# New states from 40 instead of 64 columns of keys, and two fixed double banks in PSUM

## The chip, the cores and the metric

The kernel runs on one core of a Trainium2 chip. The metric is the device time of one execution in microseconds (us). The engines are named as in the profile: PE is TensorE's matrix product, PEld its weight load (of the stationary operand), DVE is VectorE, ACT is ScalarE, POOL is GpSimd, SP is SyncE, which issues most of the DMAs. L602 is line 602 of the kernel before the change; in the changed kernel the lines after L337 stand three further down.

## The reference, cut to what matters

Two blocks follow each other. The first is an mLSTM cell over 4 batches x 8 heads (32 heads in all), 768 steps and a head width D of 40; the second a two-layer network with a quick GELU on the 3072 x 320 result.

```python
for t in range(S):                                   # per head; C is 40 x 40, n is 40
    m_new  = maximum(f_gate[t] + m, i_gate[t])
    f_stab = exp(f_gate[t] + m - m_new)
    i_stab = exp(i_gate[t] - m_new)
    C = f_stab * C + i_stab * outer(v[t], k[t])      # the state
    n = f_stab * n + i_stab * k[t]
    y[t] = sigmoid(o[t]) * (C @ q[t]) / maximum(abs(n . q[t]), 1)
x = y as (3072, 320)
h = x @ w_in                                         # w_in is 320 x 2048
out = (h * sigmoid(1.702 * h)) @ w_out               # w_out is 2048 x 320
```

All tensors are fp32.

## The kernel before

**Windows.** The 768 steps are cut into six windows of 128 steps. Within a window the cell is computed as masked attention: `scores` (L445 to L462) multiplies queries and keys into `p_s`, `weights` makes the decay factors `wt`, `values` (L485 to L519) multiplies scores by the values into `p_o` and adds in `p_i` what the state from the windows before contributes. `carry` (L595 to L612) makes the new state: for every head it multiplies the keys, transposed, by the scaled values `vw` into `p_c`, and VectorE adds that to the decayed old state. The values have one column more than D (D1 = 41, a column of ones), so the state carries C and n together.

**The state's layout.** Two heads share a column block of the state: the even head stands on partitions 0 to 39, the odd head on 64 to 103, with room for 64 each (DP = 64). In `carry` the keys are the stationary operand and the 41 columns of `vw` the moving one, so the number of key columns is the number of PSUM partitions written. The 24 columns behind a head's 40 are zeros in windows 0 and 1; from window 2 on the keys are stored densely (`k_st`) and the 24 columns are the first ones of the next head. Nothing reads what they produce: `values` takes rows 0 to 39 of each half.

**Products on tiles.** A window after the first is held in two halves of 64 steps, and the odd heads' halves are swapped, so the products of `scores`, `values` and `carry` stand on four tiles of 64 rows x 64 columns of TensorE's array, one after the other (`slot(i, x)`). `carry` of window 0 has 128 rows of keys and uses two tiles of 128 x 64. In window 5 only the first half's state is wanted, and its two products a head pair stand on two of the four tiles. An fp32 product shows as two rows of PE and two of PEld in the trace.

**Order.** Instructions are issued in the order of the program on each engine; a framework adds the semaphore waits between engines. `attention(w)` places the steps of the next window between the 16 or 14 blocks of the second product of the current one (`down` at L790, `down_fast` at L844): `carry` of both groups of 16 heads (c = 0 and c = 1) after block 3, `scores` of both some blocks later, `values` of each group in a block's place of its own, then `seam_out`, `seam_in` and `seam_turn`, which bring the result y through DRAM into the layout of the network's input xT. The first product follows (`up` at L626 and L635 in window 0, `up_fast` at L701 and L722 after it).

**PSUM.** The eight banks are two pools: `ps_m` with four single banks, and `ps_a` with two double banks. `banks(name)` at L337 takes a double bank: for the transposes `p_t`, for `p_w`, `p_cols`, `p_x`, `p_c`, `p_s`, `p_o`, `p_i` and for two pairs of rows of `p_h`. In the kernel before each call makes a new tile of the pool. Such a tile gets the double bank that was freed first, and its first writer waits until every access to the tile that had it is over.

Of the kernel before, what the change touches and what calls it, by code (L numbers as in the profile page):

```python
# [8 lines left out]
FP = mybir.dt.float32  # L9
# [17 lines left out]
def kernel(  # L27
# [13 lines left out]
    B, H, S, D = q.shape  # L41
# [6 lines left out]
    D1 = D + 1  # L48
    DP = 64
# [4 lines left out]
    PH = 2 * H  # L54
# [11 lines left out]
    ps_a = ctx.enter_context(tc.tile_pool(name="ps_a", bufs=2, space=PSUM))  # L66
# [3 lines left out]
    V, A, G, T = nc.vector, nc.scalar, nc.gpsimd, nc.tensor  # L70
# [3 lines left out]
    k_st = const.tile([L, BH * D + DP - D], FP, name="k_st")  # L74
# [20 lines left out]
    def k_of(w):  # L95
        return (k_0, k_1)[w] if w < 2 else k_st[:, 0:BH * D].rearrange("s (h d) -> s h d", d=D)

    def k_cols(w, t, h):

        return k_of(w)[t, h, :] if w < 2 else k_st[t, h * D:h * D + DP]  # L100

    def load_squares(w, what):
        for dst, src in [((k_sq, k), (q_sq, q))["kq".index(c)] for c in what]:
# [229 lines left out]
    def slot(i, x):  # L333

        return slice((x ^ i) * HL, (x ^ i) * HL + HL)

    def banks(name):  # L337
        return ps_a.tile([128, 2, 512], FP, tag="a", name=name)

    def masks():  # L340
        V.tensor_reduce(out=odd, in_=full.rearrange("p (j two) -> p two j", two=2)[:, 1], axis=AX.X, op=OP.add)
# [17 lines left out]
    def columns(w):  # L359
        if w == 0:  # L360
            pt = banks("p_cols")[:, 0, :]
            T.transpose(pt[:, 0:3 * BH], stacked[w], full)
            c = cols[w] = gate.tile([L, 4 * BH], FP, name="cols")
            A.activation(out=c[:, 2 * BH:3 * BH], in_=pt[:, 2 * BH:3 * BH], func=AF.Exp, scale=-1.0)
            return
        c = cols[w]
        A.activation(out=c[:, BH:3 * BH], in_=c[:, BH:3 * BH], func=AF.Exp, scale=-1.0)
        d = raw[w][:, 3 * BH:].rearrange("p (j i x) -> p i x j", i=2, x=2)
        for i in range(2):
            r = slice(i * 64, i * 64 + 64)  # L370
            A.activation(out=c[r, 3 * BH:].rearrange("p (x j) -> p x j", x=2), in_=d[r, i], func=AF.Exp)
# [4 lines left out]
    def transposes(w, b, between=None):  # L376
        both = ((kT, "kT", k_of(w)), (qT, "qT", q_st))[:1 if w else 2]
        for dst, name, _ in both:
            dst[w, b] = work.tile([128, NP, L], FP, tag=name, bufs=4, name=name)
        pt = banks("p_t")  # L380
        for x, (_, _, src) in enumerate(both):
            if x and between:
                between()
            for p in range(NP):
                h = b * H + 2 * p
                T.transpose(pt[:, x, p * L:(p + 1) * L], src[:, h:h + 2, :].rearrange("p a b -> p (a b)"), ident)  # L386
        for x, (dst, _, _) in enumerate(both):
            A.copy(out=dst[w, b].rearrange("r j t -> r (j t)"), in_=pt[:, x, :])
# [19 lines left out]
    def weights_begin(c):  # L408
        if c:
            both = banks("p_w")  # L410
            p_w[c] = [both[:, i, :].rearrange("s (p t) -> s p t", t=L) for i in range(2)]
        else:
            p_w[c] = [ps_m.tile([L, NP, L], FP, tag="m", name="p_w") for _ in range(2)]
        for i in range(2):
            T.matmul(p_w[c][i], ident_b, neg_mask.unsqueeze(1).to_broadcast([L, NP, L]), start=True, stop=False)
# [158 lines left out]
    def decay(w, c, x, engine=G):  # L574

        js = slice(c * NJ, (c + 1) * NJ)
        d = cols[w][:, 3 * BH + x * BH // 2:3 * BH + (x + 1) * BH // 2][:, js]
        old, dst = ((state[w % 2], state_mid), (state_mid, state[1 - w % 2]))[x]
        engine.tensor_tensor(out=dst[:, js], in0=old[:, js], in1=d.unsqueeze(2).to_broadcast([128, NJ, D1]),
                             op=OP.mult)  # L580
# [13 lines left out]
    def carry(w, c):  # L594
        js = slice(c * NJ, (c + 1) * NJ)  # L595
        pc = banks("p_c")
        n = 2 if 0 < w < NW - 1 else 1
        for j in range(NJ):
            for i in range(2):
                for x in range(n):  # L600
                    t = slot(i, x) if w else slice(0, L)
                    T.matmul(pc[i * 64:i * 64 + 64, x, j * D1:(j + 1) * D1], k_cols(w, t, c * PH + 2 * j + i),  # L602
                             vw[w, c][t, 2 * j + i, :], start=True, stop=True)
        new = lambda x: pc[:, x, 0:NJ * D1].rearrange("r (j d) -> r j d", d=D1)
        if w == 0:
            A.copy(out=state[1][:, js], in_=new(0))
            return
        for x, dst in enumerate((state_mid, state[1 - w % 2])[:n]):
            if x:
                decay(w, c, x, V)  # L610
            V.tensor_tensor(out=dst[:, js], in0=new(x), in1=dst[:, js], op=OP.add)
# [306 lines left out]
    def attention(w):  # L918
        at = (0, 1, 3, 3, 5, 6, 8, 8, 9, 12, 14) if w == 1 else (0, 0, 1, 3, 1, 4, 5, 6, 6, 10, 11)
        calls = [[(columns, w), (scale, w, 0), (scale, w, 1), (decay, w, 0, 0), (decay, w, 1, 0)],  # L920
                 [(weights, w, 0)], [(weights, w, 1)], [(carry, w, 0), (carry, w, 1)], [(open_gates, w)],
                 [(scores, w, 0), (scores, w, 1)], [(values, w, 0)], [(seam_out, w, 0), (seam_in, w, 0)],
                 [(values, w, 1), (seam_out, w, 1), (seam_in, w, 1)], [(seam_turn, w, 0)], [(seam_turn, w, 1)]]
        side = {}
        for i, c in zip(at, calls):
            side.setdefault(i, []).extend(c)
        return side

    for w in range(NW):
        more = w + 1 < NW  # L930
        if w == 0:
            for j in range(NF // 2):
                if j % 2 == 0:
                    ahead, behind = converted[j // 2]
                    run([(convert, p) for p in ahead] + [(fetch, p) for p in fetched.get(j // 2, ())])
                    up(w, j, lambda: run([(columns_turn, 1) if p is None else (convert, p) for p in behind]))
                if j == 6:
                    load(1, "o")
                if j == 1:
                    wait_for(w_in_sb[:, 1, 512:1024])  # L940
                    scale(0, 1)
                    load(1, "v")
                if j < B and j % 2:
                    carry(0, j // 2)
                if j == 3:
                    masks()
                    gates(1)
                    columns_in(1)
                if j == 4:
                    spread(1)  # L950
                    load_squares(1, "q")
                if j >= B:
                    transposes(1, j - B)
# [78 lines left out]
```

## Time and profile before

| what | us |
| --- | --- |
| time before, median of 3 runs (466.46 to 466.73) | 466.53 |
| span of the profiled execution, from the first to the last instruction | 464.1 |
| what lies around the span, by the difference of the two | 2.4 |
| PE busy (98% of the span) | 456.6 |
| PEld busy (84%) | 391.2 |
| DVE busy (75%) | 349.2 |
| ACT busy (40%) | 185.8 |
| POOL busy (35%) | 162.8 |
| mean granted TensorE clock, as a share of full speed | 0.996 |

The profile gives the profiled execution by its span alone, and a sum made against it is carried over to the median by the 2.4 us around it. The runs agree within 0.3 us. Busy time of an engine counts every moment in which at least one of its instructions runs; PE's matmuls overlap, so many short ones on several tiles count once. An engine's idle time costs only where the chain that ends last goes through it.

### The profile page before, as it was taken

What the parts mean: (1) busy time and instruction counts of PE and PEld (TensorE: products, weight loads), DVE (VectorE), ACT (ScalarE), POOL (GpSimd) and SP (SyncE); (2) the same over time, 40 slices, a digit from 0 to 9 for tenths busy, and PEclk for the clock granted to TensorE, in tenths of its full rate; (3) what the DMA queues carried; (4) which work ended last, traced back from release to release, by engine and by line L of the source; (5) the groups of instructions that cost most, each with busy time, mean ns of one, the idle gap of its engine ahead of it and who ended that gap; (6) DMA issues with size and microseconds to landing.
All of it is one profiled execution on the core that took longest, in us unless ns stands there. A gap on an engine that the chain in (4) does not pass through costs nothing.

```text
span 464.1 us, 12384 instructions
## 1 busy us (share of the span) xinstructions
PE 456.6 (98%) x5071; PEld 391.2 (84%) x5071; DVE 349.2 (75%) x738; ACT 185.8 (40%) x433; POOL 162.8 (35%) x154
## 2 busy tenths in 40 slices
PE   8999999999989999999999999999999999999996
PEld 6867877776859999779999779999888999787996
DVE  6788998799958785888786888787788766553722
ACT  5686779000536700455800354900264910164200
POOL 5101508000797700266800167610157710146200
PEclk9999999999989999999999999999999999999999
DMA  8998999049976025969024978315999305000000
GB/s 169 187 295 187 253 239 204 4 106 198 149 157 78 3 59 123 200 113 189 9 58 107 194 119 162 53 33 125 175 140 156 63 18 140 29 1 1 1 28 30
DMA packets 135561, 52.87 MB, mean 114 GB/s; under 512 B 101984, under 2 KB 131632, under 8 KB 135504
## 3 DMA queue, kind: packets, MB, share of 16 engines
q1 hardware_dynamic: 127136, 50.27, 55.4%
q10 hardware_dynamic: 8048, 1.66, 1.8%
q8 instruction: 40, 0.66, 0.6%
q0 software_dynamic: 320, 0.15, 0.2%
q14 instruction: 17, 0.14, 0.1%
HBM read 44.52 MB, written 7.54 MB: 112 GB/s over the span
## 4 chain that ended last, share of the span: by engine, by line
PE 88%; SPq 4%; DMA 2%; issue 2%; DVE 2%; POOL 1%; ACT 1%; DVEq 0%; POOLq 0%; ACTq 0%
PE p_out L844 33%; PE p_h L722 24%; PE p_out L790 8%; PE p_h L701 7%; PE p_h L626 5%; SPq L122 3%; PE p_c L602 3%; PE p_o L503 2%; PE p_s L459 2%; PE p_i L511 2%; DMA s_in<-in_moe_w_in_dram 2%; PE p_h L635 2%; POOL g L781 1%; SPq L167 0%; PE p_t L386 0%
## 5 line engine op out<-in xcount | busy, mean ns | idle before, releaser
L781 POOL TENSOR_TENSOR g<-g,parts 128x512 f32<-128x512 f32 x30 | 38.2, 1272 | 196.5 <-ACT g L739 187.7
L761 ACT COPY parts<-p_h 128x256 f32<-128x256 f32 x40 | 14.9, 372 | 164.5 <-PE p_h L722 134.1
L844 PE MATMUL p_out<-w_out_sb,g 128*128 128x160 f32 x480 | 68.9, 300 | 0.0
L722 PE MATMUL p_h<-xT,w_in_sb 128*128 128x256 f32 x240 | 66.4, 385 | 2.0 <-ACT g L739 2.0
L844 PEld LDWEIGHTS p_out<-w_out_sb,g 128*128 128x128 f32 x480 | 66.4, 190 | 0.5
L690 ACT ACTIVATE g<-g 128x512 f32<-128x512 f32 x80 | 47.8, 629 | 30.1 <-DVE g L775 19.1
L722 PEld LDWEIGHTS p_h<-xT,w_in_sb 128*128 128x128 f32 x240 | 44.9, 191 | 14.2 <-issue 5.5
L849 DVE TENSOR_TENSOR o_sb<-o_sb,p_out 128x160 f32<-128x160 f32 x70 | 21.4, 317 | 44.2 <-PE p_out L844 43.6
L844 PE MATMUL p_out<-t_sb,s 128*128 128x160 f32 x320 | 47.1, 300 | 0.0
L844 PEld LDWEIGHTS p_out<-t_sb,s 128*128 128x128 f32 x320 | 44.4, 190 | 0.2
L722 PE MATMUL p_h<-t_x,s_in 128*128 128x256 f32 x160 | 42.0, 385 | 0.0
L435 ACT ACTIVATE wt<-wt,cols 128x64 f32<-128x64 f32 x160 | 38.8, 334 | 0.1
L701 PE MATMUL p_h<-xT,w_in_x 64*128 64x512 f32 (+1 forms) x200 | 37.1, 514 | 0.0
L790 PE MATMUL p_out<-w_out_sb,g 128*128 128x320 f32 x128 | 35.7, 436 | 0.0
L722 PEld LDWEIGHTS p_h<-t_x,s_in 128*128 128x128 f32 x160 | 31.0, 194 | 4.4
L762 DVE TENSOR_TENSOR t_x<-p_h,parts 128x256 f32<-128x256 f32 x40 | 16.9, 424 | 20.3 <-PE p_h L722 12.9
L790 PEld LDWEIGHTS p_out<-w_out_sb,g 128*128 128x128 f32 x128 | 23.9, 190 | 9.6
L701 PEld LDWEIGHTS p_h<-xT,w_in_x 64*128 64x128 f32 x200 | 18.5, 186 | 14.9 <-issue 13.9
L739 ACT COPY g<-p_h 128x512 f32<-128x512 f32 x30 | 17.5, 582 | 31.1 <-PE p_h L701 17.5
L626 PE MATMUL p_h<-xT,w_in_sb 128*128 128x256 f32 x128 | 29.6, 384 | 0.0
L775 DVE TENSOR_TENSOR g<-p_h,parts 128x512 f32<-128x512 f32 x40 | 27.6, 691 | 1.4
L626 PEld LDWEIGHTS p_h<-xT,w_in_sb 128*128 128x128 f32 x128 | 23.6, 190 | 5.3 <-issue 2.4
(205 smaller groups left out, 853.6 us busy)
## 6 DMA issues: line engine op xcount, KB each, us to landing
q_sq<-in_q_dram SPq DMA_DIRECT2D x20, 320.0 KB, 10.6
wt<-m_row SPq DMA_DIRECT2D x20, 256.0 KB, 5.4
k_sq<-in_k_dram SPq DMA_DIRECT2D x16, 320.0 KB, 6.0
out_dram<-o_sb SPq DMA_DIRECT2D x24, 160.0 KB, 1.9
eo<-in_o_gate_dram SPq DMA_DIRECT2D x5, 640.0 KB, 7.9
bits<-in_moe_w_in_dram SPq DMA_DIRECT2D x6, 512.0 KB, 11.3
q_sq<-x_row SPq DMA_DIRECT2D x10, 256.0 KB, 3.0
v_st<-in_v_dram SPq DMA_DIRECT2D x14, 160.0 KB, 5.7
```

The lines of the kernel that those rows point to most:

```text
L435: A.activation(out=x[:, h, :], in_=x[:, h, :], func=AF.Exp, scale=-1.0, bias=cols[w][:, c * PH + h:c * PH + h + 1])
L626: T.matmul(ph[j][i][:, t], w_in_sb[:, c, f * 128:(f + 1) * 128], x[:, c, t], start=(first and c == 0 and n == 0), stop=(not first and c == ...
L690: A.activation(out=gs[w, j][:, i, :], in_=gs[w, j][:, i, :], func=AF.Gelu_apprx_sigmoid)
L701: T.matmul(row[:, t], w_in_x[r, j, :], xT[w][r, 2].rearrange("p b t -> p (b t)")[:, t], start=(start and h == 0), stop=(not start and h == ...
L722: T.matmul(out, a, x[n], start=start, stop=stop)
L739: A.copy(out=g[:, 0, :], in_=row0)
L762: V.tensor_tensor(out=u2, in0=p56[:, right], in1=y[:, left], op=OP.add)
L775: V.tensor_tensor(out=g[:, 1, :], in0=row1, in1=y[:, half_w:3 * half_w], op=OP.add)
L781: G.tensor_tensor(out=g0, in0=g0, in1=u, op=OP.add)
L790: T.matmul(po, gs[w, f // 2][:, f % 2, b * L:(b + 1) * L], w_out_sb[:, f, :], start=(f == 0), stop=(f == NF - 1))
L844: T.matmul(po, a(f), b[:, f, :], start=(f == 0), stop=(f == NH - 1))
L849: V.tensor_tensor(out=dst, in0=x, in1=po, op=OP.add)
```

## The change

Two edits. `carry` passes 40 columns of keys to the product in place of 64 and writes 40 partitions in place of 64, in all windows. And `banks` no longer makes tiles: `ps_a` holds two fixed tiles from the start, and the calls take them in turn. Waits then follow from which parts of a fixed tile an instruction reads and writes, and the n-th call's double bank no longer depends on which was freed first. VectorE's and ScalarE's reads of `p_c` still cover all 128 partitions; partitions 40 to 63 and 104 to 127 hold what an earlier use of the bank left there.

```diff
     def k_cols(w, t, h):
 
-        return k_of(w)[t, h, :] if w < 2 else k_st[t, h * D:h * D + DP]
+        return k_of(w)[t, h, 0:D] if w < 2 else k_st[t, h * D:h * D + D]
...
+    halves = [ps_a.tile([128, 2, 512], FP, tag=f"a{i}", bufs=1, name=f"p_a{i}") for i in range(2)]
+
     def banks(name):
-        return ps_a.tile([128, 2, 512], FP, tag="a", name=name)
+        halves.reverse()
+        return halves[0]
...
                 for x in range(n):
                     t = slot(i, x) if w else slice(0, L)
-                    T.matmul(pc[i * 64:i * 64 + 64, x, j * D1:(j + 1) * D1], k_cols(w, t, c * PH + 2 * j + i),
+                    T.matmul(pc[i * 64:i * 64 + D, x, j * D1:(j + 1) * D1], k_cols(w, t, c * PH + 2 * j + i),
                              vw[w, c][t, 2 * j + i, :], start=True, stop=True)
```

## The prediction

> **What bounds the kernel now.** I read the page's totals first, then PE's waits, the chain that ended last around a carry, the carry's own rows, and last VectorE's order after it.
>
> ```profile
> PE 456.6 (98%) x5071; PEld 391.2 (84%) x5071; DVE 349.2 (75%) x738; ACT 185.8 (40%) x433; POOL 162.8 (35%) x154
> ...
> PE 88%; SPq 4%; DMA 2%; issue 2%; DVE 2%; POOL 1%; ACT 1%; DVEq 0%; POOLq 0%; ACTq 0%
> ```
>
> PE is the bound: 98% busy, 88% of the chain. Until 30.96 us the chain is DMA, ScalarE and VectorE (the first weights), and PE's own arrival there is only 0.08 us early. After that PE stands still for something else once, 2.0 us before 134.29 (a chain over VectorE and POOL that PE's L701 at 112.7 starts, so it moves with PE). A nanosecond less in a PE burst after 30.96 is therefore a nanosecond less at the end, unless PE then meets a wait that does not move. The waits of PE's weight loads name the candidate:
>
> ```profile
> PEld p_c L602 <- issue: 1.8, 7, 0.4
> PEld p_o L503 <- issue: 1.3, 6, 0.4
> PEld p_s L459 <- issue: 1.1, 5, 0.4
> PEld p_o L503 <- DVE wt L462: 1.0, 4, 0.4
> ```
>
> `p_o` waits for VectorE's product L462 in four cases. The chain in the window 150 to 165 us shows where that lies:
>
> ```profile
> 154.00 2.01 PE p_c L602 x128
> 156.01 2.37 PE p_out L844 x16
> 158.38 2.02 PE p_s L459 x128
> 160.41 2.37 PE p_out L844 x16
> 162.78 1.11 PE p_o L503 x60
> ```
>
> **The burst of a carry.** The rows of line 602, and those of `p_s`:
>
> ```profile
> L602 PEld LDWEIGHTS p_c<-vw,k_st x448: 129/135/135, 153.9 to 369.5; 64*64 64x64 f32 x150
> L602 PE MATMUL p_c<-vw,k_st x448: 227/227/248, 153.9 to 369.5; 64*64 64x41 f32 x150
> ...
> L448 PEld LDWEIGHTS p_s<-qT,kT x64: 183/188/188, 8.2 to 20.4; 40*128 40x128 f32 x64
> ```
>
> And the stretches with a carry in them (us; busy and rows of PE and PEld; clock, DMA share, GB/s):
>
> ```profile
> 34.70:35.90 1.20, 1.10 (x32) 1.01 (x32) 1.00 1.10 333
> ...
> 74.70:76.90 2.20, 2.08 (x128) 1.96 (x128) 1.00 1.10 319
> 153.90:156.10 2.20, 2.08 (x128) 1.96 (x128) 1.00 0.02 7
> ...
> 367.60:369.90 2.30, 2.06 (x64) 1.94 (x64) 1.00 0.03 7
> ```
>
> 128 rows on four tiles take as long as 64 rows on two, and 32 rows on two tiles half of that. So it is not the number of instructions that sets the pace but one tile's own round: 128/4 = 64/2 = 32 rounds, and 16. The single records repeat on one tile every 58.3 ns, at full clock. Which side of the round is it? The moving side: where nothing but the moving operand can be the limit, records of `p_out` with 160 columns follow each other every 135.9 ns and those of `p_h` with 256 every 215.8, so a column costs 79.9/96 = 0.83 ns and a matmul 2.5 ns on top; 41 columns are 36.7 ns, and `p_s`, with 64 columns on four tiles, repeats every 58.5, 2.5 ns more than this rate gives. With the same surcharge `p_c` would need 39.3 ns. It takes 58.3, so something else limits it. The stationary side: 64 columns load in 135 ns and 128 in 188, 0.83 ns a column; 64 columns are 53 ns of a round, and 5 ns are left as in `p_s`. I take it that the 64 stationary columns set the 58.3.
>
> **What 40 columns change.** 24 columns x 0.83 = 19.9 ns off the load give 38.4; the moving side then holds at 39.3. A round drops by 19.0 ns. No row has a stationary operand of fewer than 64 columns, so the bounds are 39.3 (rate holds) and 58.3 (a tile's load costs 64 columns whatever it holds, or a round has a floor); I take 39.3, because 64 and 128 columns differ by just the rate. Instructions don't stand in the way: inside `p_s` four tiles' pairs are issued within 27 ns.
>
> - Window 0: two bursts of 16 rounds, 2 x 0.30 = 0.61 us of PE.
> - Windows 1 to 5: 32 rounds each, 0.61 us each; the first half (c = 0) 0.30.
>
> That is 3.65 us of PE, all on the path. What arrives is less, because of the next waits.
>
> **Windows 2 to 4.** VectorE after the carry at 153.9, in order of time:
>
> ```profile
> 155.22 0.50 DVE L611 TENSOR_TENSOR state_mid<-p_c,state_mid 128x328 f32<-128x328 f32 x1 [0.85 <-PE p_c L602]
> ...
> 161.38 2.34 DVE L462 TENSOR_TENSOR wt<-p_s,wt 128x1024 f32<-128x1024 f32 x2
> ```
>
> From 155.22, where it waits for the c = 0 half, to 163.72 VectorE has no idle time: state sums, the network's sums, two L849, two L462. PE's `p_i` at 163.78 takes a double bank that the second L462 frees, 0.04 us earlier. So this stretch is VectorE's, and it starts as soon as c = 0 is done: 0.30 us earlier, not 0.61. Each of the three windows gives 0.30, in all 0.91; the rest turns into a longer wait at L503. Everything later in the window starts from `values` and moves along.
>
> **Window 1.** VectorE's row is full from an input DMA on:
>
> ```profile
> 75.71 4.00 DVE L394 STREAM_TRANSPOSE qT<-q_sq 128x512 f32<-128x512 f32 x4 [1.16 <-DMA q_sq<-in_q_dram]
> ...
> 87.61 2.35 DVE L462 TENSOR_TENSOR wt<-p_s,wt 128x1024 f32<-128x1024 f32 x2
> ```
>
> It ends at 89.96; PE's `p_i` starts at 90.92. Windows 0 and 1 bring PE 1.22 us forward, but if the landing of `q_sq` stays where it is, PE can gain only 0.95 less 0.04 = 0.91 here. I take 0.91; if the landing moves along (ScalarE's conversions before it stand behind PE's results), up to 1.22.
>
> **Window 5.** VectorE has one state sum fewer, and `p_o` at 376.43 finds L462 done 1.8 us before. The whole 0.61 counts.
>
> **The fixed tiles.** The order on every engine is the same; of the waits written into the program only PE's differ. Most that go or come point at work long done: nothing either way. Two matter. `p_cols` at 11.36 now takes the double bank of `p_w`, which ScalarE frees at 11.47, where the `p_t` behind it waited before: 0.11 us later, all before 30.96, of which the 0.08 us of PE's spare arrival covers most; 0 to 0.1 us, I take 0. And `p_o` of c = 1 now waits for L518 instead of L517: 93.83 against a start at 94.32, and 0.5 us of room in the other windows too, with both hanging on the same `p_i`: nothing; queued behind it would be all of PE. If L518 were later by more than 0.5 us, the excess would count five times.
>
> **The sum.** 0.91 + 0.91 + 0.61 = 2.43 us off a span of 464.1: 461.7, and with the 2.4 us around it 464.1 against the median of 466.53. About 0.2% (0.93 us) is what a measurement of this kernel tells from no change.
>
> The Trainium skill, "TensorEngine Tiling (Array Packing)", Instruction Overhead, speaks against the change: a matmul carries some 60 cycles, and a free dimension of 1 costs as much as one of 60. No row here moves fewer than 41 columns. Read as a floor of 60 moving columns in fp32 it would hold a round at an estimated 55 ns, and the sum would be 0.4 us in place of 2.43. "TensorE: Matmul & The Clock Gate", LDWEIGHTS, says the load goes by columns, P/1.2 ns: 53 ns for 64, as the rows have it, and an estimated 33 for 40, with which the sum stays.
>
> **The rivals.**
>
> *A, forecast, 0.60:* rounds of about 39 ns; 464.1. Between 463.4 (the landing moves too, and rounds of 36.7 without the tiles' surcharge save 21.6 ns: 2 x 0.69 + 3 x 0.34 + 0.69 = 3.1) and 464.9 (rounds of 44 save three quarters, 1.8, and 0.1 goes at the start).
>
> *B, half-way, 0.12:* some pace between 39.3 and 58.3 holds the rounds near 49. Half of 0.61 in windows 0, 1 and 5 and half of 0.91 in 2 to 4: 0.92 + 0.45 = 1.37, so 465.2. For it: no row on one tile repeats faster than 54 ns. Against: nothing shown needs that long for 41 columns.
>
> *C, no gain, 0.18:* the narrow load costs as much as a wide one, since tile and instruction count stay. 466.5. For it: loads of 40 and of 64 rows take the same 135 ns, so what is left empty can be paid for; against: rows are the other side of the array.
>
> *D, slower, 0.10:* a product that fills only 40 of a tile's 64 columns loses the overlap between tiles, and the bursts run tile by tile. Place: the 2.0 us of each carry. Price if a round doubles: 192 rounds x 58.3 = 11.2 us, 477.7. It decides the sign from a round of 58.3 + 0.93/192 = 63.1 ns on. Against: `p_i`, with 40 of 64 rows, keeps the pace of `p_o` with 64 (14.5 ns a row in both).
>
> **How the numbers follow.** Range: A's lower end, then over B to just past C, leaving out D, half of C and A's fringe: 463.4 to 466.6. Faster by over 0.2%: A and most of B, 0.70. Within 0.2%: C and the rest of B, 0.20. Slower: 0.10.
>
> **What would show it.** Right: a carry of 64 or 128 rows with PE busy for about 1.5 us instead of 2.08, loads of L605 at about 115 ns instead of 135, a longer wait of `p_o` for L462 in windows 2 to 4, and VectorE's first L611 about 0.3 us closer to the carry's start. Wrong: bursts of 2.0 us as before, or a `p_o` of c = 1 that waits for L518.

## The result and the profile after

| what | before | after |
| --- | --- | --- |
| median of nine runs each, side by side (us) | 466.55 | 464.18 |
| lowest and highest (us) | 465.49, 471.27 | 462.75, 465.24 |
| ratio of the times, with its 95% interval (the two medians alone give 0.9949) | | 0.9934 [0.9905, 0.9963] |
| span of the profiled execution (us) | 464.1 | 462.5 |
| time of the profiled execution (us) | not given | 464.2 |
| PE busy (us) | 456.6 | 454.0 |

The forecast of 464.1 lies 0.1 us from the median. That is closer than its reasons deserve. The two profiled spans differ by 1.57 us, not by the 2.43 us of the sum, and a repetition of the same kernel with 12 runs against 23 (cols_40 below) gave a ratio of 0.9965 [0.9951, 0.998], 1.6 us. I take 1.6 us as what the change brings; one of the prediction's three terms did not arrive. Some executions, of either kernel, run 3.4 us after 134 us at half the granted clock and others don't: of 23 of the kernel before, 15 have a mean clock of 0.995 or 0.996 (median 466.17 us) and 8 one of 0.998 or more (464.85), so single times and small sets of runs scatter by over 1 us, and what follows goes by positions within one profile. The two profiled executions above both have it.

The page of the changed kernel, totals and chain, to be held against the first fence of the prediction:

```profile
PE 454.0 (98%) x5071; PEld 387.3 (84%) x5071; DVE 352.7 (76%) x738; ACT 185.8 (40%) x433; POOL 162.9 (35%) x154
...
PE 88%; DVE 6%; issue 2%; POOL 1%; DMA 1%; ACT 1%; SPq 0%; DVEq 0%; POOLq 0%
```

PE has 2.6 us less to do, and no instruction went. VectorE, which has the same 738 instructions on the same data, is busy 3.5 us longer, and its share of the chain went from 2% to 6%. That is where the missing gain is to be looked for.

The carry's rows (duration as least/median/longest, ns) and its stretches (us; busy and rows of PE and of PEld; clock, DMA share, GB/s), after:

```profile
L605 PEld LDWEIGHTS p_a<-vw,k_st x448: 109/115/121, 153.0 to 367.9; 64*40 64x40 f32 x150
L605 PE MATMUL p_a<-vw,k_st x448: 195/199/228, 153.0 to 368.0; 64*40 64x41 f32 x150
```

```profile
34.80:36.00 1.20, 0.81 (x32) 0.69 (x32) 1.00 1.42 236
74.20:76.40 2.20, 1.48 (x128) 1.36 (x128) 1.00 1.16 317
152.90:155.10 2.20, 1.46 (x128) 1.34 (x128) 1.00 0.03 7
366.70:369.00 2.30, 1.43 (x64) 1.31 (x64) 1.00 0.03 7
```

The load takes 115 ns, as forecast, and a carry 1.46 us where it took 2.08. From first to last load record a burst of 128 rows went from 1.823 to 1.228 us: 0.595 over 31 rounds is 19.2 ns, so a round takes 39.1 ns. This half of the prediction stands in every window.

Now the window 150 to 165 us, as the chain of waits has it after the change (start, length, what):

```profile
153.07 0.80 PE p_a L605 x64
...
153.96 0.51 DVE state_mid L614
...
154.57 1.49 DVE state L582
...
158.11 1.21 PE p_a L462 x64
...
160.45 1.22 DVE wt L465
...
161.72 1.24 PE p_a L506 x64
```

Before, this chain ran over PE alone. Now it leaves PE when the c = 0 half of the carry is done and goes through VectorE twice. PE's waits after (us in all, times, longest):

```profile
PEld p_a L462 <- DVE state L614: 1.5, 6, 0.3
...
PEld p_a L506 <- DVE wt L465: 1.0, 3, 0.3
```

The second of these was there before, about as long (1.0 us in four cases, then called `p_o` and L462). The first is new: now the scores of c = 1 also wait, for VectorE's state sum that frees their double bank. And VectorE's own order, after (start, busy, operation, idle time before it):

```profile
153.96 0.50 DVE L614 TENSOR_TENSOR state_mid<-p_a,state_mid 128x328 f32<-128x328 f32 x1 [0.53 <-PE p_a L605]
154.57 1.48 DVE L582 TENSOR_TENSOR state<-state_mid,cols 128x328 f32<-128x328 f32 x1
...
157.02 0.50 DVE L582 TENSOR_TENSOR state<-state_mid,cols 128x328 f32<-128x328 f32 x1
```

The first sum comes 0.32 us sooner after the carry's start (0.53 instead of 0.85 us of waiting), just as forecast. But the decay behind it, the same multiplication that takes 0.50 us at 157.02, takes 1.48 us. Before the change it took 1.16, in the same place, and 0.50 for its twin:

```profile
155.82 1.16 DVE L579 TENSOR_TENSOR state<-state_mid,cols 128x328 f32<-128x328 f32 x1
...
157.95 0.50 DVE L579 TENSOR_TENSOR state<-state_mid,cols 128x328 f32<-128x328 f32 x1
```

And POOL at the same time, first after and then before:

```profile
153.35 2.35 POOL L442 TENSOR_SCALAR_AFFINE_SELECT wt<-wt 64x1024 f32<-64x1024 f32 x2
```

```profile
154.28 2.35 POOL L439 TENSOR_SCALAR_AFFINE_SELECT wt<-wt 64x1024 f32<-64x1024 f32 x2
```

POOL's two selects, the causal masks of the weights, end at 155.70 after and at 156.63 before. The held decay ends at 156.05 and 156.98: 0.35 us later in both. What VectorE gained ahead of the decay it lost inside it.

Window by window, from the carry's first record to `p_i` of c = 0 (us), the quantity by which the experiments are read from here on:

| kernel | window 1 | windows 2, 3, 4 | window 5 |
| --- | --- | --- | --- |
| before | 16.15 | 9.85, 9.84, 9.84 | 9.72 |
| after | 15.56 | 9.85, 9.84, 9.84 | 9.08 |

0.6 us in windows 1 and 5, nothing in the three between.

### The profile page after: what moved, and what is told of

Its sections match the earlier page's. It is cut to its first block, busy times and chain, and to the rows that moved or that the text cites. A ratio compares the mean times of both kernels' runs of the same rounds, so it can differ in the third digit from the quotient of the medians.

```text
span 462.5 us, 12372 instructions
## 1 busy us (share of the span) xinstructions
PE 454.0 (98%) x5071; PEld 387.3 (84%) x5071; DVE 352.7 (76%) x738; ACT 185.8 (40%) x433; POOL 162.9 (35%) x154
## 4 chain that ended last, share of the span: by engine, by line
PE 88%; DVE 6%; issue 2%; POOL 1%; DMA 1%; ACT 1%; SPq 0%; DVEq 0%; POOLq 0%
PE p_out L847 31%; PE p_h L725 18%; PE p_out L793 8%; PE p_a L725 7%; PE p_h L629 6%; PE p_h L704 4%; PE p_a L704 3%; PE p_a L506 2%; PE p_a L514 2%; PE p_h L638 2%; PE p_a L462 2%; PE p_a L605 1%; DVE state L582 1%; PE p_a L389 1%; PE p_s L451 1%
## 5 line engine op out<-in xcount | busy, mean ns | idle before, releaser
L693 ACT ACTIVATE g<-g 128x512 f32<-128x512 f32 x80 | 47.8, 630 | 30.1 <-DVE g L778 19.2
L725 PE MATMUL p_h<-xT,w_in_sb 128*128 128x256 f32 x160 | 45.8, 389 | 2.0 <-ACT g L742 2.0
L725 PEld LDWEIGHTS p_h<-xT,w_in_sb 128*128 128x128 f32 x160 | 29.6, 191 | 12.1 <-issue 5.5
L629 PE MATMUL p_h<-xT,w_in_sb 128*128 128x256 f32 x128 | 29.6, 384 | 0.0
L629 PEld LDWEIGHTS p_h<-xT,w_in_sb 128*128 128x128 f32 x128 | 23.6, 190 | 5.3 <-issue 2.4
L442 POOL TENSOR_SCALAR_AFFINE_SELECT wt<-wt 64x1024 f32<-64x1024 f32 x20 | 24.4, 1221 | 6.1 <-ACT wt L438 5.4
L815 POOL TENSOR_TENSOR g<-g 128x512 f32<-128x512 f32 x20 | 25.5, 1274 | 0.0
L832 DVE TENSOR_TENSOR s<-g,s 128x256 f32<-128x256 f32 x40 | 24.2, 644 | 0.0
L847 PE MATMUL p_out<-t_sb,g 128*128 128x160 f32 x160 | 23.8, 302 | 0.0
```

The lines of the kernel that those rows point to most:

```text
L442: G.affine_select(out=r, in_=r, compare_op=OP.is_ge, fill=0.0, base=0, pattern=[[0, PH], [1, HL]], channel_multiplier=-1)
L629: T.matmul(ph[j][i][:, t], w_in_sb[:, c, f * 128:(f + 1) * 128], x[:, c, t], start=(first and c == 0 and n == 0), stop=(not first and c == ...
L693: A.activation(out=gs[w, j][:, i, :], in_=gs[w, j][:, i, :], func=AF.Gelu_apprx_sigmoid)
L725: T.matmul(out, a, x[n], start=start, stop=stop)
L815: G.tensor_tensor(out=a10, in0=a00, in1=a10, op=OP.subtract)
L832: V.tensor_tensor(out=s2, in0=hidden(w, j + 4, 0)[:, :, c], in1=s2, op=OP.subtract)
```

## The experiments

My theory after the result: rounds are as forecast, the fixed tiles cost nothing, and in windows 2 to 4 POOL's selects hold VectorE, so that `p_i` and the scores of c = 1 are late by what PE gained. The rivals: the fixed tiles take back part of the gain; VectorE's long decay has to do with PE's access to PSUM; or the missing part is only scatter between executions. Comparisons are with the kernel before, run beside it on the same chip.

### The columns and the tiles apart

cols_40 is the changed kernel again, unedited.

> The changed kernel once more, for comparison on one chip. By the profiles of before and after, whose stretches from carry to p_i are 16.12 and 15.53 us in window 1, 9.84 and 9.84 in windows 2 to 4, 9.69 and 9.05 in window 5: about 1.6 us below the kernel before, not the 2.4 forecast. If the forecast's terms for windows 2 to 4 were right and the profile of after only disturbed: 2.4, and stretches of 9.54 there.

Measured: 463.93 us against 466.05, ratio 0.9965 [0.9951, 0.998]; stretches 16.26, then 10.58, 9.85, 9.85, then 9.08. Windows 3 to 5 repeat those of after. In window 2 the carry came 1.02 us sooner than in after (151.98 against 153.00), VectorE and POOL met in another order, and the stretch was 0.73 longer: most of a head start is lost there again. In window 1 PE's loads stood for 0.60 us before the carry's last load, and the profile shows nothing that they waited for; hence 16.26. Only 3 of these 12 executions had the half clock after 134 us, against 15 of the 23 beside them. Like against like the gain is 1.65 us with it (464.52 against 466.17) and 1.04 without (463.81 against 464.85), so 1.6 us is no firmer than that.

tiles_64 keeps the fixed tiles and puts the 64 columns back:

```diff
-        return k_of(w)[t, h, 0:D] if w < 2 else k_st[t, h * D:h * D + D]
+        return k_of(w)[t, h, :] if w < 2 else k_st[t, h * D:h * D + DP]
...
-                    T.matmul(pc[i * 64:i * 64 + D, x, ...
+                    T.matmul(pc[i * 64:i * 64 + 64, x, ...
```

> The two fixed tiles alone, with 64 columns of keys as before. Theory (the columns are all of it): carry bursts as before, 2.0 us for 128 rows, loads of 135 ns; the stretch from a carry's first load to the start of p_i of c = 0 stays at 9.84 us in windows 2 to 4, 16.1 in window 1 and 9.69 in window 5; time 0 to 0.1 us above the kernel before. Rival (the fixed tiles' other waits bring part of the gain): 0.5 us or more below the kernel before, with the stretches or the first 31 us shorter.

Measured: 466.36 us, ratio 1.0013 [1.0003, 1.0022]; stretches 16.15, then 9.85, 9.85, 9.85, then 9.72: those of before. Nothing in the windows costs the 0.3 us that the median shows. All eleven executions had the half clock; against the 15 before that had it too (466.17), 0.2 us are left. PE's work in the first product begins later in that execution (31.65 us against 30.96), which could have been the wait of `p_cols` at 11.4 us. So the same kernel was run again as tiles_64b, beside tiles_64_flip, in which `p_cols` takes the other bank:

```diff
-            pt = banks("p_cols")[:, 0, :]
+            pt = halves[0][:, 0, :]
```

> tiles_64 once more, since it came out 0.3 us above the kernel before by medians and 0.6 by the ratio, where 0 to 0.1 was expected, with all of the profile's difference before 31.65 us. Theory (the input DMAs' arrival in the first 12 us differs from execution to execution): time within 0.2 us of the kernel before or scattered like it, stretches unchanged. Rival (the fixed tiles cost that much at the start): again 0.3 to 0.6 us above, with PE's first L638 at 31.5 us or later.

> tiles_64 with p_cols in the double bank that is free first, as in the kernel before. Theory (p_cols's wait for ScalarE is the whole cost of the fixed tiles, at most 0.1 us): 0 to 0.1 us below tiles_64b. Rival (that wait is the 0.3 to 0.6 us): 0.3 or more below tiles_64b.

Measured: 465.94 us each, ratios 0.9997 [0.9986, 1.0008] and 0.9994 [0.9985, 1.0002]; in tiles_64b the stretches are those of before. (The profiled execution of tiles_64_flip took 671.51 us and is not read.) The 0.3 us did not repeat, although the first product began late in tiles_64b as well, at 31.51 us, and the other bank brings nothing that can be told from none. In all profiles read the first product begins somewhere between 30.80 and 31.89 us; no_select_64 below, with the pool's own tiles, is at 31.08 like after. The fixed tiles cost nothing that these runs can measure. 40 columns without the fixed tiles were not tried.

### What sets a round

widths gives each window its own number of columns (with 32, window 3 leaves 8 columns of the keys out of the state):

```diff
+        m = (40, 48, 56, 32, 64, 40)[w]
-        return k_of(w)[t, h, 0:D] if w < 2 else k_st[t, h * D:h * D + D]
+        return k_of(w)[t, h, 0:m] if w < 2 else k_st[t, h * D:h * D + m]
...
-                    T.matmul(pc[i * 64:i * 64 + D, x, ...
+                    T.matmul(pc[i * 64:i * 64 + (40, 48, 56, 32, 64, 40)[w], x, ...
```

> The changed kernel with another number of key columns in each window's carry: 40, 48, 56, 32, 64, 40 for windows 0 to 5 (window 3 leaves 8 columns of the keys out of the state). Theory (a round is the longer of the stationary side, 0.83 ns a column, and the moving side, 41 columns, each with about 5 ns on top): loads of 115, 122, 128, 108, 135 ns; bursts of 128 rows with rounds of 45 (48 columns), 52 (56), 39 (32), 58 (64); window 5's 64 rows on two tiles with rounds of 39 (40). Rival (a step, or a floor of its own at 39): 48 and 56 columns have rounds of 39 or 58, nothing between; 32 columns below 39 if the moving side is not the limit there.

Measured, by rows (mean ns and count before the idle time), here two of its widths:

```profile
L606 PEld LDWEIGHTS p_a<-vw,k_st 64*64 64x64 f32 x128 | 2.0, 135 | 0.2 <-issue 0.2
...
L606 PEld LDWEIGHTS p_a<-vw,k_st 64*56 64x56 f32 x128 | 1.7, 128 | 0.2 <-issue 0.2
```

| columns | load, median ns | burst, us | same burst with 40 columns | round, ns |
| --- | --- | --- | --- | --- |
| 32 (window 3) | 105 | 1.180 | 1.228 | 37.6 |
| 40 | 115 | 1.228 | 1.228 | 39.1 |
| 48 (window 1) | 122 | 1.409 | 1.252 | 44.2 |
| 56 (window 2) | 128 | 1.617 | 1.228 | 51.6 |
| 64 (window 4) | 135 | 1.823 | 1.228 | 58.3 |

(round: 39.1 ns plus the difference of the two bursts over 31 rounds.) From 56 to 64 a column costs 6.7/8 = 0.84 ns, from 48 to 56 0.93; from 40 to 32 the whole step is worth 1.5 ns. So above 40 columns the stationary side sets the round, and at 40 it has all but stopped doing so. The expectation had 39 ns and a load of 108 for 32 columns. That the 41 moving columns hold the 37.6 is worked out from the pace of `p_out` and `p_h` (36.7 ns in the prediction) and not shown by itself, as no run varied them. A fixed floor, rival C's or that of 60 moving columns, would have shown one pace for all; there is none down to 37.6 ns.

### Who holds VectorE

no_select_64 is the kernel before without POOL's selects, that is without the causal mask, in windows 2 to 5; no_select_40 is the changed kernel with the same edit. Like widths and memset_40 they ran once each, and are read by their windows:

```diff
-        for i in range(2):
+        for i in range(2 if w == 1 else 0):
```

> The kernel before without POOL's selects of the weights in windows 2 to 5 (the causal mask is left out there). Theory of the hold: VectorE's decay L579 in the carry takes 0.50 us instead of 1.16, L829 0.60 instead of 0.82 and 1.35; PE meets no wait between carry and p_i: stretch 9.69 us in windows 2 to 4. Rival (the decay is slow for another reason): 1.16 us as before, stretch 9.84.

> The changed kernel without POOL's selects of the weights in windows 2 to 5 (the causal mask is left out there). Theory of the hold: decay L582 0.50 us instead of 1.48, stretches of 9.07 us in windows 2 to 4, 0.61 below no_select_64, so the full forecast of the burst arrives once the selects are away; span about 1.8 us below no_select_64 over windows 2 to 4 and 5 together with 0.61 of window 5, 3.4 in all with windows 0 and 1. Rival: stretches equal to those of no_select_64.

Measured: spans 463.8 and 459.1. VectorE in window 3 of no_select_40:

```profile
223.31 0.50 DVE L614 TENSOR_TENSOR state_mid<-p_a,state_mid 128x328 f32<-128x328 f32 x1 [0.53 <-PE p_a L605]
223.92 0.50 DVE L582 TENSOR_TENSOR state<-state_mid,cols 128x328 f32<-128x328 f32 x1
```

The decay is 0.50 us in both kernels, and the chain lies on PE alone again, in no_select_40 so:

```profile
222.42 1.39 PE p_a L605 x125
223.81 2.37 PE p_out L847 x16
226.18 2.02 PE p_a L462 x128
228.21 2.37 PE p_out L847 x16
230.58 1.07 PE p_a L506 x64
```

Stretches of windows 2, 3, 4: 9.73 three times with 64 columns, 9.20, 9.11, 9.11 with 40. So without the selects the whole 0.62 us arrives in windows 3 and 4, as in window 5, and before the change the selects cost only 9.84 - 9.73 = 0.11 us a window. The two spans differ by 4.7 us where 3.4 was expected; only the one with 64 columns had the half clock after 134 us, and I don't read more into it.

Is it that POOL is busy, or that it reads? memset_40 puts a write without a read in the selects' place, with 0.5 for all weights of windows 2 to 5:

```diff
+            if w > 1:
+                G.memset(r, 0.5)
+                continue
```

> The changed kernel with POOL filling the weights with a constant in place of the select, in windows 2 to 5 (weights and mask are left out there): POOL writes the same tiles at the same place but reads none. Theory 1 (what holds VectorE is POOL's reading): decay 0.50 us, stretches of 9.07. Theory 2 (any access of POOL holds it): the decay ends about 0.34 us after POOL's fill, and is longer than 0.9 us where the two overlap that long.

Measured: span 459.3, stretches 9.11 in all three windows. POOL and VectorE in window 3:

```profile
222.92 1.95 POOL L443 MEMSET wt<- 64x1024 f32 x2
```

```profile
224.15 0.50 DVE L585 TENSOR_TENSOR state<-state_mid,cols 128x328 f32<-128x328 f32 x1
```

The decay runs in the middle of POOL's write (222.92 to 224.87) and takes its 0.50 us. So what holds it, as far as select and memset tell, is a POOL instruction that reads SBUF. The decay itself reads two operands from SBUF; the sums of L614, with one operand from PSUM, take 0.50 us beside the select too (153.96 in the fence of after, while the select ran). The Trainium skill states this pair: "SBUF — State Buffer", Who interferes with whom, has VectorE instructions with two SBUF inputs contend with GpSimd instructions that read SBUF, and not with those that only write, since the second input comes through a shared read interface. The 1.48, 0.50 and 0.50 us agree.

Which of the two is held? In windows 2 to 4 of after, the decay starts 0.01 to 0.02 us behind the second select, in window 2 at 154.57 (above) against:

```profile
154.56 1.14 POOL L442 TENSOR_SCALAR_AFFINE_SELECT wt<-wt 64x1024 f32<-64x1024 f32 x1
```

In window 3 of widths, which has 32 columns and keeps the selects, it starts 0.02 us ahead. Then it takes its 0.50 us and the select 1.49 instead of 1.14:

```profile
225.20 0.50 DVE L583 TENSOR_TENSOR state<-state_mid,cols 128x328 f32<-128x328 f32 x1
```

```profile
225.22 1.49 POOL L443 TENSOR_SCALAR_AFFINE_SELECT wt<-wt 64x1024 f32<-64x1024 f32 x1
```

The stretch there is 9.07 us, with the selects in place. So whichever starts first runs and the other one waits, and the three lost gains hung on a few hundredths of a microsecond.

### Taking the wait away

sums_late moves VectorE's L832 of two column blocks, held likewise (0.82 and 1.35 us where 0.42 is its time alone), behind the next product:

```diff
-                lambda: (last_sums(w, c, (2, 3)), product(total(1), t1, (o11, o10), (o01, o01))),
-                lambda: (product(block(1, 1), t4, (o10, o10)), store(1)),
+                lambda: product(total(1), t1, (o11, o10), (o01, o01)),
+                lambda: (last_sums(w, c, (2, 3)), product(block(1, 1), t4, (o10, o10)), store(1)),
```

> The changed kernel with two sums of the network (L832, c = 0 and 1, j = 2 and 3) moved on VectorE from before the scores' products to behind them. Theory (POOL's selects of weights hold VectorE's additions and products of two SBUF operands back, first the decay L582, then L832): the second hold no longer stands before L465, L465 of c = 1 ends about 0.6 us earlier, p_i no longer waits, stretches in windows 2 to 4 of about 9.25 us (PE's 9.07 and the 0.18 that scores of c = 1 still wait for the state sum), 1.8 us below cols_40 at most, 1.0 if L465 is held otherwise. Rival (p_i is held by something before VectorE, as POOL's second select itself): stretches of 9.84 as before, time as cols_40.

Measured: 463.51 us, ratio 0.995 [0.9934, 0.9965]; stretches 9.52, 9.53, 9.52: 0.32 us won a window, not 0.6. `p_i` is free, but the scores of c = 1 still wait, 2.28 us from their first to their last record against 1.88 without the wait, because the held decay still stands ahead of the sum that frees their bank. The expectation had put this second wait at 0.18 us; it is 0.40.

best puts both sums of the middle state ahead of the decays, so that the banks are freed before VectorE can be held, and has the edits of sums_late and tiles_64_flip:

```diff
-        for x, dst in enumerate((state_mid, state[1 - w % 2])[:n]):
-            if x:
-                decay(w, c, x, V)
-            V.tensor_tensor(out=dst[:, js], in0=new(x), in1=dst[:, js], op=OP.add)
+        added[c] = new
+        V.tensor_tensor(out=state_mid[:, js], in0=new(0), in1=state_mid[:, js], op=OP.add)
...
+    def carry_end(w, c):
...
+        decay(w, c, 1, V)
+        V.tensor_tensor(out=dst[:, js], in0=added[c](1), in1=dst[:, js], op=OP.add)
...
-                 [(weights, w, 0)], [(weights, w, 1)], [(carry, w, 0), (carry, w, 1)], [(open_gates, w)],
+                 [(weights, w, 0)], [(weights, w, 1)], [(carry, w, 0), (carry, w, 1), (carry_end, w, 0), (carry_end, w, 1)], [(open_gates, w)],
```

> sums_late, and VectorE adds the first half's state for both groups of heads before it decays either, so that the held decay has work in front of it, and p_cols takes the double bank that is free first. Theory: state sums end about 0.5 us earlier, PE's 0.18 us before the scores of c = 1 goes, stretches of 9.07 us in windows 2 to 4, and 0.1 us less in the first 31 us: 2.3 to 2.4 us below cols_40 by spans. Rival (no hold; VectorE's time is just used up): stretches of 9.5 or more.

Measured: 462.09 us, ratio 0.9928 [0.9913, 0.9942], 1.8 us below cols_40 run beside it (2.3 to 2.4 were expected): it beats both kernels. Stretches 9.11, 9.11, 9.11, as without any select. VectorE in window 3:

```profile
224.36 1.11 DVE L612 TENSOR_TENSOR state_mid<-p_a,state_mid 128x328 f32<-128x328 f32 x2 [0.53 <-PE p_a L605]
225.39 1.05 DVE L582 TENSOR_TENSOR state<-state_mid,cols 128x328 f32<-128x328 f32 x1
226.47 0.50 DVE L622 TENSOR_TENSOR state<-p_a,state 128x328 f32<-128x328 f32 x1
```

The decay is still held, 1.05 us, but nobody waits for it; the chain in that window is PE's alone. Of PE's two waits shown above, the one for `wt` is gone from the list, and the one for the state sum is down from 1.5 to 0.3 us.

best_64 is best with 64 columns (the edit of tiles_64):

> best with 64 columns of keys. Theory (with VectorE's order mended, PE is the limit between carry and p_i with 64 and with 40 columns): stretches of 9.73 us in windows 2 to 4 against best's 9.11, each 0.61 longer, and 3.5 us above best by spans, start apart: the forecast's full burst. Rival (the columns bring only 1.6 to 2.4 us here too): stretches less than 0.4 us longer than best's.

Measured: 465.68 us, ratio 0.9994 [0.9975, 1.0013]. best lies 3.6 us below it by medians of two sets of runs, beside which the kernel before took 466.05 and 466.07, and 3.6 us by spans; but best's profiled execution had the half clock after 134 us and that of best_64 had not. The undisturbed window 3 has 9.73 against 9.11: the 0.62 us that PE gained. In windows 2 and 4 of best_64 the stretch is 10.58 and 10.57, and in best it is 9.11; so the 3.6 us are not the columns alone. In window 2 the clock goes with it: the three profiles that have selects and no half clock (cols_40, widths, best_64) show 10.57 or 10.58 there, and none of the six that have both does. Window 4 of best_64 is open.

## Why the prediction was right, and where it was not

- **The burst** (58.3 to 39.3 ns, by the stationary side): right; 39.1 measured, and the widths confirm the rate and the change of side. The bursts shown above refute C, "no gain", B, the half-way pace, and D, the lost overlap.
- **Windows 0 and 1** (0.91 us): 0.93, by luck of two errors. The landing of `q_sq` was not the anchor: VectorE's transposes start at 74.85 instead of 75.71 and no longer wait for it, and `p_i` starts at 89.81 instead of 90.92. With the first product 0.12 us later in this execution that is PE's whole 1.23 us, the "up to 1.22" of the prediction. Of it 0.18 us was lost again before the next carry, which comes 0.93 us sooner; which work gave it back was not tested.
- **Windows 2 to 4** (0.91 us): 0.00. This is the step that failed. From 155.22 to 163.72 VectorE "has no idle time", and the prediction took that for work that moves as a block once the c = 0 half is done. It was not all work: 0.66 us of the first decay (1.16 against 0.50) and some 1.3 us of the two L829 were time held by POOL. A hold ends with POOL's instruction, so as long as the select starts first, 0.32 us earlier at the head is 0.32 us longer inside. The two durations of one form stood a few lines apart in the view the prediction quoted from, and it cut them out. Hence its sign of a "longer wait at L503" was wrong too: that wait kept its 1.0 us, and a new one came up at the scores.
- **Window 5** (0.61 us): 0.64 (carry 0.93 us sooner, `p_i` 1.57). It has no held decay on the path.
- **The fixed tiles** (0): right within what the runs can tell; no `p_o` of c = 1 is seen waiting for L521, the former L518.
- **The sum**: 0.93 + 0.00 + 0.64 = 1.57 us, the difference of the spans, 0.86 less than forecast. That 464.1 was met all the same is luck, the work of a second mis-sized term, the 2.4 us around the span. In after it is 464.2 - 462.5 = 1.7 us, and 1.7 in tiles_64, cols_40 and best as well. The profiled execution of before, with a span of 464.1, was then an execution of about 465.8, some 0.7 us shorter than the median it was carried over to. 461.7 + 1.7 would have been 463.4, below the median by nearly the gain that did not come. That median itself mixes four executions with the half clock (464.8) and five without (463.31).

## What to carry to other kernels

Before an engine's unbroken row is read as work, compare the durations of one form within the row: where the same instruction takes 0.50 us and 1.16 us, the difference can be a wait that no list of waits shows, and it is anchored to the engine that causes it. When such a wait lies between two engines, put the instructions that others wait for ahead of those that can be held; here that brought 1.8 us on top of the 40 columns, and nothing without them. For short products on tiles, work out the round from both operands' columns and cut the longer side until they meet; only the stationary side was varied here.

## What the runs showed of the hardware that was not expected

- A VectorE multiplication with two operands in SBUF that starts behind a POOL select stands: 0.50 us becomes 1.16 or 1.48, ending 0.35 us after the select's end. Where it starts 0.02 us ahead it takes 0.50, and the select 1.49 instead of 1.14. Beside a POOL memset it takes 0.50.
- A stand of PE of 2.04 us before 133.4 us costs 1.7 us up to the next carry or nothing, by where it falls. In the profiles that show the half clock after it, the granted clock is full for 129.71 us, which is 38 times 3.413, and then half for 3.41. Count steps of 3.413 us from the moment at which the clock becomes full (3.85 us in after, 3.74 in cols_40). Where the whole stand lies in one step, 2.04 to 2.07 us of it, as in seven profiles, the next step has half the clock. In the five others (tiles_64_flip left out) the grid cuts the stand, at most 1.95 us of it lie in one step, and the clock stays full. After, two such steps (us; busy and rows of PE, PEld, DVE, ACT, POOL; clock, DMA share, GB/s):

```profile
130.14:133.55 3.41, 1.37 (x7) 0.38 (x4) 3.03 (x4) 1.10 (x2) 3.41 (x3) 1.00 0.22 82
133.55:136.97 3.42, 3.42 (x9) 2.67 (x9) 0.62 (x2) 0.90 (x2) 3.42 (x3) 0.50 0.93 239
```

The same kernel as cols_40:

```profile
130.04:133.45 3.41, 1.91 (x10) 0.58 (x6) 3.38 (x5) 0.58 (x2) 3.41 (x4) 1.00 0.20 64
133.45:136.86 3.41, 2.83 (x13) 2.53 (x14) 1.44 (x4) 1.43 (x4) 3.41 (x2) 1.00 0.89 244
```

From the end of the stand to the next carry it is 19.64 us in after (133.36 to 153.00) and 17.95 in cols_40 (134.03 to 151.98): 1.69 us, half of 3.41. "TensorE: Matmul & The Clock Gate", Part 1, has the clock fall after an idle window of some 3.4 us which runs free of the kernel. The steps of 3.41 us agree with that; but a step did not have to be idle throughout: 2.04 us of it were enough here, and 1.95 (best_64) were not.
